# Expert rows kept as planes of half words and turned into columns by the load's DMA transpose, instead of by TensorE

## The chip, the cores and the metric

The kernel runs on one core of a Trainium2 chip as one launch. The metric is the device time of one execution in microseconds (us); the time of before is the median of three runs. Besides, one execution was recorded by the profiler, and every duration below comes from that one. Engines carry the names of the profile: PE is TensorE (PEld its weight loads), ACT is ScalarE, DVE is VectorE, POOL is GpSimd, SP is SyncE, which here only issues DMAs.

## The reference, cut to what matters

```python
x = attention(q, k, v)                     # 4 batches x 576 tokens, 8 heads of 64: 2304 rows of 512
x = (x @ w_a) * (x @ w_b) @ w_out          # 512 -> 1536 -> 512
en = expert_emb / (norm(expert_emb) + 1e-6)            # 8 experts
logits = (x / (norm(x) + 1e-6)) @ en.T / tau
expert_idx = argmax(logits, axis=1)
gate_w = softmax(logits)[rows, expert_idx]
for e in range(8):
    mask = expert_idx == e
    out[mask] = gate_w[mask, None] * (relu(x[mask] @ w1[e]) @ w2[e])   # 512 -> 1024 -> 512
```

All of it is fp32. The kernel gets fp32 products out of three matmuls each: an operand is split into a high part (rounded, `fp32r`) and a low part (what the rounding left), and `mm3` adds high x high, high x low and low x high.

## The kernel before

**Stages.** Four blocks of tokens pass through attention and the first feed-forward part (`f_step`, twelve steps per block, and `x1_run` for the product with `w_out`); the attention of the next block is woven into the steps of the current one. While a block's steps run, the rows of the block before it are routed (`Router`): logits on DVE, the choice of the expert, the rank within the expert on PE, and then `scatter`, an indirect DMA from POOL that puts each token's row into the DRAM table `xs` at a slot of its expert. A row there is 521 words: 512 of x, 8 logit differences, the token's number. The last block is done in columns (`x1_last`: twelve steps for 512 tokens, twelve for the other 256); its routers `ra` (4 tiles of 128 tokens) and `rb` (2 tiles) get the rows by matmuls against an identity, `row_out` copies them from PSUM with ACT.

**The experts** (`Moe2`) come in the order of their load, with capacities of 384, 352, 336, 320, 304, 288, 272 and 256 tokens. For one expert `x_load` brings the rows back as `xr` (tokens on the partitions), and `x_prep` makes columns of them: PE transposes 128x128 pieces against the identity into PSUM (`x_trans`, L1052), `split` makes the high part `xTh` with ACT (L679) and the low part `xTl` with DVE (L680). For expert 0 this is `x_early` (256 tokens, while block 3 still runs) and `x_rest`. `h_full` multiplies with w1 (eight pieces, into PSUM tiles `hp`, three buffers), `y_part` or, for the experts in `TURNED`, `yt_part` with w2. `y_out` scales by the gate and scatters to the output. `gate_sq` takes the sum of squares of each row tile with ACT's Square (L1085), `gate` makes the inverse norm on DVE and the softmax's sum with one Exp on ACT (L1094).

**Order.** The program's order is written by hand and each engine works through its own instructions in that order; nothing is rescheduled. SP issues every load in one queue: weight pieces of 512 KB (`w_load`), four ahead of the one that `w_split` takes apart, and the rows of expert e+2 (`x_load`) when expert e is done. `GATE_AT` says behind which `yt_part` the gate's instructions stand, `XPREP` which columns of the next expert are made behind which.

Of the kernel before, what the change touches and what calls it, by code (L numbers as in the profile page):

```python
# [12 lines left out]
U32 = mybir.dt.uint32  # L13
AF = mybir.ActivationFunctionType
# [5 lines left out]
E, F2 = 8, 1024  # L20
# [17 lines left out]
GATE_AT = 0  # L38
# [6 lines left out]
RW = DM + E + 1  # L45
C_DL = DM
C_IDX = DM + E
# [13 lines left out]
MASK_OF = {0: 0, 2: 2, 4: 3, 6: 4, 7: 5}  # L61

# [20 lines left out]
def fused_kernel(ctx: ExitStack, tc: tile.TileContext, qk, v, wab, wout, w1, w2, emb, tau, cst, msk, out, dbg=None):  # L83
# [5 lines left out]
    xs = dram.tile([E * RS, RW], F32, name="xs")  # L89
# [78 lines left out]
    def make_empty():  # L168
        empty = rbox[0][:, NTT:NTT + 1, :]
        nc.gpsimd.memset(empty, 0.0)  # L170
        nc.gpsimd.memset(empty[:, :, C_IDX:], SENT)
        return empty

    def prefill(empty, e):
        nc.sync.dma_start(
            out=xs[e * RS:e * RS + CAP, :].rearrange("(t p) c -> p t c", p=128),
            in_=empty.to_broadcast([128, NCT, RW]),
        )
# [5 lines left out]
    class Router:  # L184
        def __init__(self, tile0, nt, rows, x, ps, tags):
# [20 lines left out]

        def row_out(self, t, h):
            p = self.pr.pop((t, h))
# [61 lines left out]
        def scatter(self, t):  # L270
            i = nc.gpsimd.indirect_dma_start(
                out=xs, out_offset=bass.IndirectOffsetOnAxis(ap=self.di[:, t:t + 1], axis=0),
                in_=self.rows[:, t, :], in_offset=None,
# [7 lines left out]
        def steps(self, per):  # L281
# [9 lines left out]
            for _ in range(3):  # L291
                yield
# [684 lines left out]
    class Moe2:  # L977
# [4 lines left out]
        def __init__(self):  # L982
# [4 lines left out]
            self.xr, self.ixi, self.xT, self.hT, self.sq, self.gates = {}, {}, {}, {}, {}, {}  # L987
# [46 lines left out]
        def x_load(self, e, t0=0, t1=None):  # L1034
# [3 lines left out]
            if e not in self.xr:  # L1038
                self.xr[e] = self.mr.tile([128, NCT, RW], F32, tag="xr", name="xr", bufs=2)[:, :self.nct(e), :]
# [3 lines left out]
                self.sq[e] = rt.tile([128, NCT], F32, tag="sq", name="sq")[:, :self.nct(e)]  # L1043
                self.gates[e] = self.mr.tile([128, NCT], F32, tag="gate", name="gate", bufs=3)[:, :self.nct(e)]
            nc.sync.dma_start(
                out=self.xr[e][:, t0:t1, :], in_=xs3[self.expert(e), 128 * t0:128 * t1, :].rearrange("o (t p) c -> p (o t) c", p=128))

        def x_ids(self, e, t0, t1):
            nc.vector.tensor_copy(out=self.ixi[e][:, t0:t1], in_=self.xr[e][:, t0:t1, C_IDX])

        def x_trans(self, e, tp, d, t, c):
            nc.tensor.transpose(tp[:, c:c + 128], self.xr[e][:, t, 128 * d:128 * d + 128], ident)  # L1052

        def x_prep(self, e, ds):
            if e >= E:
                return
            if 0 in ds:
                self.x_ids(e, 0, self.nct(e))
            for d in ds:
                if e == 1:  # L1060
                    tp = self.pt.tile([128, CAP], F32, tag="hp", name="xtq", bufs=3)
                else:
                    tp = self.pt.tile([128, 512], F32, tag="xtp", name="xtp")
                for t in range(self.nct(e)):
                    self.x_trans(e, tp, d, t, 128 * t)
                split(tp[:, :CAPS[e]], self.xT[e][0][:, d, :], self.xT[e][1][:, d, :])

        def x_early(self, h):
            tp = ps.tile([128, 2, EARLY], F32, tag=f"mm{2 + h}", name="xte")
            for d in range(2):  # L1070
                for t in range(EARLY // 128):
                    self.x_trans(0, tp[:, d, :], 2 * h + d, t, 128 * t)
            split(tp, *[x[:, 2 * h:2 * h + 2, :EARLY] for x in self.xT[0]])

        def x_rest(self):
            m = CAPS[0] - EARLY
            tp = self.pt.tile([128, 4, 128], F32, tag="xtp", name="xtr")[:, :, :m]
            for d in range(4):
                self.x_trans(0, tp[:, d, :], d, EARLY // 128, 0)
            split(tp, *[x[:, :, EARLY:] for x in self.xT[0]])  # L1080

        def gate_sq(self, e, t):
            if t < self.nct(e):
                jk = self.mr.tile([128, DM], BF16, tag="jk", name="jk")
                nc.scalar.activation(out=jk, in_=self.xr[e][:, t, :DM], func=AF.Square, accum_out=self.sq[e][:, t:t + 1])  # L1085

        def gate(self, e):
            n = self.nct(e)
            sh = [128, n, E]
            ri = inv_norm(self.sq[e], 128, n)  # L1090
            dl = rt.tile([128, NCT, E], F32, tag="dl", name="dl")[:, :n, :]
            g = self.gates[e]
            nc.vector.tensor_tensor(out=dl, in0=self.xr[e][:, :, C_DL:C_DL + E], in1=ri.unsqueeze(2).to_broadcast(sh), op=ALU.mult)
# [3 lines left out]
            nc.vector.reciprocal(out=g, in_=g)  # L1097

# [41 lines left out]

        def h_full(self, e):
            c0, c1 = 0, CAPS[e]
            for f in range(8):
# [4 lines left out]
                if 1 <= f <= 3:  # L1148
                    self.yt_turn(e - 1, f - 1)
                    self.gate_sq(e, f - 1)  # L1150
                if f == 5 and e not in TURNED:
                    self.gate(e)
# [49 lines left out]
        def run(self):  # L1202
# [3 lines left out]
            for t in range(self.nct(0)):  # L1206
                self.gate_sq(0, t)
            self.h_rest()
            self.gate(0)
            for e in range(E):  # L1210
# [3 lines left out]
                if e in TURNED:  # L1214
                    for d in range(4):
# [3 lines left out]
                        if d == GATE_AT:  # L1219
                            self.gate(e)  # L1220
# [381 lines left out]
```

## Time and profile before

| | |
|---|---|
| time, median of 3 runs | 782.15 us (780.53 to 783.88) |
| the profiled execution: its time | 778.46 us |
| the profiled execution: its span | 776.6 us |
[...]
| PE busy | 765.0 us, 99% |
| DVE, ACT, POOL busy | 507.9, 403.1, 206.1 us |
| DMA | 138.45 MB, mean 178 GB/s |

The span runs from the first to the last instruction; the 1.9 us between it and the execution's time lie around it. A share of busy time says how full an engine is on average, not whether something waits for it.

### The profile page before, as it was taken

The numbers are of one execution on the slowest core, as the hardware profiler recorded it, in microseconds if no ns is written. First come the engines' busy times: TensorE is split into PE (matmuls) and PEld (weight loads), VectorE is DVE, ScalarE is ACT, GpSimd is POOL, SyncE is SP. The second block draws the span as 40 slices with busy tenths as digits, with TensorE's granted clock in tenths as the row PEclk, the third lists the DMA queues.
The fourth block names the chain that finished last, engine by engine and source line by source line (L and its number), as shares of the span: only waits on it lengthen the run. The fifth ranks groups of instructions, "written<-read, shape, count | busy, mean of one in ns | idle before, by whom it ended". The sixth has DMA issues, their size and how long they took to land.

```text
span 776.6 us, 14562 instructions
## 1 busy us (share of the span) xinstructions
PE 765.0 (99%) x5503; PEld 683.0 (88%) x5503; DVE 507.9 (65%) x1072; ACT 403.1 (52%) x945; POOL 206.1 (27%) x228
## 2 busy tenths in 40 slices
PE   7999999999999999999999999999999999999997
PEld 4799998888788888888899998899897999999995
DVE  4788878758895388975376743355565565665672
ACT  5776764367642366642333332455463554755761
POOL 3634443023521234342032324421011000101111
PEclk9999999999999999999999999999999999999999
DMA  9968779478752433213512123444574545645621
GB/s 353 370 223 274 247 272 336 147 274 285 287 193 81 164 116 132 83 55 100 173 55 82 55 82 144 184 138 162 210 252 161 184 155 167 231 154 197 234 81 37
DMA packets 40672, 138.45 MB, mean 178 GB/s; under 512 B 4082, under 2 KB 4338, under 8 KB 38160
## 3 DMA queue, kind: packets, MB, share of 16 engines
q1 hardware_dynamic: 37504, 127.90, 48.0%
q0 software_dynamic: 3088, 9.52, 3.2%
q8 instruction: 45, 0.74, 0.4%
q14 instruction: 35, 0.29, 0.1%
HBM read 112.03 MB, written 25.80 MB: 177 GB/s over the span
## 4 chain that ended last, share of the span: by engine, by line
PE 86%; issue 5%; DMA 4%; DVE 2%; ACT 1%; POOL 1%; POOLq 0%; DVEq 0%; ACTq 0%
PE mm L721 13%; PE mm L723 12%; PE mm L722 12%; PE xr L721 4%; PE xr L723 4%; PE xr L722 4%; DMA out_dram<-yo,ixi 4%; PE hp L721 3%; PE hp L723 3%; PE hp L722 3%; PE xm L721 2%; PE xm L723 2%; PE xm L722 2%; PE ytp L723 2%; PE ytp L722 2%
## 5 line engine op out<-in xcount | busy, mean ns | idle before, releaser
L721 PE MATMUL mm<-x0h,ab 128*128 128x288 f32 (+2 forms) x480 | 171.1, 357 | 0.0
L723 PE MATMUL mm<-x0h,ab 128*128 128x288 f32 (+2 forms) x480 | 166.9, 348 | 0.2 <-DVE ab L680 0.2
L722 PE MATMUL mm<-x0l,ab 128*128 128x288 f32 (+2 forms) x480 | 166.8, 347 | 0.2 <-DVE x0l L506 0.2
L680 DVE TENSOR_TENSOR wl<-raw,wh 128x1024 fp32r<-128x1024 f32 x60 | 73.0, 1222 | 53.6 <-ACT wh L679 53.5
L776 POOL TENSOR_TENSOR gl<-g,gh 128x288 fp32r<-128x288 f32 (+2 forms) x60 | 82.2, 1370 | 84.9 <-ACT gh L775 81.5
L721 PEld LDWEIGHTS mm<-x0h,ab 128*128 128x128 f32 x480 | 90.2, 188 | 10.0
L723 PEld LDWEIGHTS mm<-x0h,ab 128*128 128x128 f32 x480 | 90.1, 188 | 9.6 <-DVE ab L680 0.4
L722 PEld LDWEIGHTS mm<-x0l,ab 128*128 128x128 f32 x480 | 90.2, 188 | 8.5 <-DVE x0l L506 0.5
L680 DVE TENSOR_TENSOR wo<-wor,wo 128x512 fp32r<-128x512 f32 x60 | 43.9, 731 | 58.2 <-ACT wo L679 54.5
L679 ACT ACTIVATE wo<-wor 128x512 fp32r<-128x512 f32 x60 | 37.9, 631 | 84.4 <-PE xr L723 52.7
L1192 POOL DMA_INDIRECT out_dram<-yo,ixi x23 | 24.4, 1062 | 207.6 <-ACT yo L1191 164.7
L680 DVE TENSOR_TENSOR ab<-abr,ab 128x1024 fp32r<-128x1024 f32 x45 | 59.3, 1318 | 24.9 <-ACT ab L679 24.9
L772 DVE TENSOR_TENSOR g<-a,mm 128x288 f32<-128x288 f32 (+2 forms) x72 | 39.5, 549 | 51.8 <-PE mm L723 42.0
L721 PE MATMUL hp<-xTh,wh 128*128 128x352 f32 (+6 forms) x224 | 69.0, 308 | 0.0
L723 PE MATMUL hp<-xTh,wl 128*128 128x352 f32 (+6 forms) x224 | 67.7, 302 | 0.0
L722 PE MATMUL hp<-xTl,wh 128*128 128x352 f32 (+6 forms) x224 | 67.6, 302 | 0.0
L679 ACT ACTIVATE wh<-raw 128x1024 fp32r<-128x1024 f32 x64 | 67.0, 1054 | 0.0
L775 ACT ACTIVATE gh<-g 128x288 fp32r<-128x288 f32 (+2 forms) x60 | 33.1, 552 | 57.5 <-DVE g L772 57.5
L679 ACT ACTIVATE ab<-abr 128x1024 fp32r<-128x1024 f32 (+1 forms) x53 | 50.6, 961 | 17.5 <-PE mm L723 11.9
L223 DVE SCALAR_TENSOR_TENSOR jl<-rows,en_a 128x512 bf16<-128x512 f32 x60 | 56.2, 937 | 1.2
L721 PE MATMUL xr<-wo,gh 128*128 128x512 f32 x144 | 56.4, 392 | 0.0
L723 PE MATMUL xr<-wo,gl 128*128 128x512 f32 x144 | 56.1, 390 | 0.0
(262 smaller groups left out, 1793.0 us busy)
## 6 DMA issues: line engine op xcount, KB each, us to landing
raw<-in_w_dram SPq DMA_DIRECT2D x64, 512.0 KB
abr<-wab SPq DMA_DIRECT2D x36, 512.0 KB
wor<-wout SPq DMA_DIRECT2D x24, 512.0 KB
qkt<-in_qk_dram SPq DMA_DIRECT2D x12, 832.0 KB
vt<-in_v_dram SPq DMA_DIRECT2D x12, 768.0 KB
c<-in_wab_dram SPq DMA_DIRECT2D x8, 1024.0 KB
xs<-rows SPq DMA_DIRECT2D x8, 781.5 KB
wab<-abr SPq DMA_DIRECT2D x12, 512.0 KB
```

Of the source, the lines that this page charges most:

```text
L223: nc.vector.scalar_tensor_tensor(out=jl, in0=self.rows[:, t, :DM], scalar=1.0, in1=ebox[e // E1][:, e % E1, :], op0=ALU.mult, op1=ALU.mult ...
L679: nc.scalar.activation(out=hi, in_=raw, func=AF.Copy)
L680: (eng or nc.vector).tensor_tensor(out=lo, in0=raw, in1=hi.bitcast(F32), op=ALU.subtract)
L721: nc.tensor.matmul(out=out_, lhsT=lh, rhs=rh, start=first, stop=False)
L722: nc.tensor.matmul(out=out_, lhsT=lh, rhs=rl, start=False, stop=False)
L723: nc.tensor.matmul(out=out_, lhsT=ll, rhs=rh, start=False, stop=last)
L772: nc.vector.tensor_tensor(out=g, in0=kept[hf], in1=acc[1, hf], op=ALU.mult)
L775: nc.scalar.activation(out=hi, in_=g, func=AF.Copy)
L776: nc.gpsimd.tensor_tensor(out=lo, in0=g, in1=hi.bitcast(F32), op=ALU.subtract)
L1192: nc.gpsimd.indirect_dma_start(out=out, out_offset=bass.IndirectOffsetOnAxis(ap=self.ixi[e][:m, t:t + 1], axis=0), in_=yo[:m, :], in_offse ...
```

## The change

A row in `xs` has 524 words now. Its 512 words of x stand as two planes of 16-bit halves: 512 low halves, then 512 high halves. Behind them come the logit differences, two words for the sum of squares (`C_SQ`), the token's number and one spare word. `x_load` issues a DMA transpose of the planes, which puts them as columns into `pl` (128 partitions, 8 groups, tokens), and a small DMA for the 12 words behind (`tl`). `x_join` puts the halves together again with one ACT copy of 16-bit elements into `xf`, and `split` takes the parts from there. The TensorE transposes and their PSUM tiles go.

On the side of the rows, POOL writes the planes of a tile into the neighbouring slot of the row buffer (`planes`), ACT takes the squares (`square`), and `scatter` first copies the 12 words to that slot. In `rb` ACT writes the planes straight from PSUM. `gate` is cut in two: its DVE part stands behind the first `yt_part`, its Exp and the rest behind the third. `x_early` moves from steps 17 and 20 of `x1_last` to steps 9 and 11.

```diff
-GATE_AT = 0
+GATE_AT = (0, 2)
-RW = DM + E + 1
+RW = DM + E + 4
 C_DL = DM
-C_IDX = DM + E
+C_SQ = DM + E
+C_IDX = DM + E + 2
+PLANE_AT = (21, 23, 25, 27)
...
+        def square_row(self, t):
+            if self.x is None:
+                junk = self.stage[t][:, :DM // 2].bitcast(BF16)
+            else:
+                junk = rt.tile([128, DM], BF16, tag="jl", name="jl", bufs=1)
+            self.square(t, self.rows[:, t, :DM], 0, junk)
+
+        def planes(self, t, eng):
+            out = self.stage[t % len(self.stage)][:, :DM].bitcast(U16).rearrange("p (w c) -> p w c", w=2)
+            in_ = self.rows[:, t, :DM].bitcast(U16).rearrange("p (c w) -> p w c", w=2)
...
+                eng.tensor_copy(out=out, in_=in_)
...
         def row_out(self, t, h):
+            halves = self.rows[:, t, :DM].bitcast(U16).rearrange("p (w k c) -> p w k c", w=2, k=4)
             nc.scalar.activation(
-                out=self.rows[:, t, 256 * h:256 * h + 256].rearrange("p (k c) -> p k c", k=2),
-                in_=p[:, :, :128], func=AF.Copy)
+                out=halves[:, :, 2 * h:2 * h + 2, :],
+                in_=p.bitcast(U16).rearrange("p k (c w) -> p w k c", w=2), func=AF.Copy)
+            jl = rt.tile([128, DM], BF16, tag="jl", name="jl", bufs=1)
+            self.square(t, p, h, jl[:, :256])
...
         def logit(self, i):
             t, e = divmod(i, E)
+            if i in PLANE_AT:
+                q = PLANE_AT.index(i)
+                self.square_row(q)
+                self.planes(q, nc.gpsimd)
...
         def scatter(self, t):
+            row = self.rows[:, t, :]
+            if self.stage:
+                row = self.stage[t % len(self.stage)]
+                nc.gpsimd.tensor_copy(out=row[:, DM:], in_=self.rows[:, t, DM:])
...
+            r0, r1 = 128 * t0, min(128 * t1, CAPS[e])
+            nc.sync.dma_start_transpose(
+                out=self.pl[e][:, :, r0:r1], in_=xs3[self.expert(e), r0:r1, :DM].bitcast(U16).rearrange("o r c -> (o r) c"))
             nc.sync.dma_start(
-                out=self.xr[e][:, t0:t1, :], in_=xs3[self.expert(e), 128 * t0:128 * t1, :].rearrange("o (t p) c -> p (o t) c", p=128))
+                out=self.tl[e][:, t0:t1, :], in_=xs3[self.expert(e), 128 * t0:128 * t1, DM:].bitcast(F32).rearrange("o (t p) c -> p (o t) c", p=128))
...
-        def x_trans(self, e, tp, d, t, c):
-            nc.tensor.transpose(tp[:, c:c + 128], self.xr[e][:, t, 128 * d:128 * d + 128], ident)
+        def x_join(self, e, d0, d1, r0, r1):
+            n = d1 - d0
+            x = self.mr.tile([128, 2 * CAP], U32, tag="xf", name="xf", bufs=2)[:, :n * (r1 - r0)]
+            x = x.rearrange("p (d c) -> p d c", d=n)
+            words = x.bitcast(U16).rearrange("p d (c w) -> p w d c", w=2)
+            planes = self.pl[e].rearrange("p (w d) c -> p w d c", w=2)[:, :, d0:d1, r0:r1]
+            nc.scalar.activation(out=words, in_=planes, func=AF.Copy)
+            split(x.bitcast(F32), *[y[:, d0:d1, r0:r1] for y in self.xT[e]])
...
-        def gate_sq(self, e, t):
-            if t < self.nct(e):
-                jk = self.mr.tile([128, DM], BF16, tag="jk", name="jk")
-                nc.scalar.activation(out=jk, in_=self.xr[e][:, t, :DM], func=AF.Square, accum_out=self.sq[e][:, t:t + 1])
...
+                    if 15 <= i < 15 + ha:
+                        ra.square_row(i - 15)
+                        ra.planes(i - 15, nc.gpsimd)
-                    if i == 18:
-                        for t in range(ha):
-                            ra.scatter(t)
-                    if i in (17, 20):
-                        moe.x_early((i - 17) // 3)
+                    if 18 <= i < 18 + ha:
+                        ra.scatter(i - 18)
+                    if i in (9, 11):
+                        moe.x_early((i - 9) // 2)
```

Three places show what stands where. PE, in expert 1's products with w2 (`yp`), where the columns of expert 2 are made; before:

```order
L723 MATMUL yp<-wh,hTl 128x512
L1052 MATMUL xtp<-ident,xr 128x128 x6
L721 MATMUL yp<-wh,hTh 128x512
L722 MATMUL yp<-wl,hTh 128x512
L723 MATMUL yp<-wh,hTl 128x512
```

and there is nothing in place of the six transposes afterwards:

```order
L764 MATMUL yp<-wh,hTl 128x512
L762 MATMUL yp<-wh,hTh 128x512
L763 MATMUL yp<-wl,hTh 128x512
L764 MATMUL yp<-wh,hTl 128x512
L762 MATMUL yp<-wh,hTh 128x512
```

The transposes have left PE's list. SP's queue, where expert 0 is done: `raw` are weight pieces, `xr` the rows of expert 2; before:

```order
L1010 DMA raw<-in_w_dram 128x1024
L1010 ISA
L1010 DMA raw<-in_w_dram 128x1024
L1045 ISA
L1045 DMA xr<-xs 128x3x521
L1010 ISA
L1010 DMA raw<-in_w_dram 128x1024
```

and afterwards, at the same place, with `pl` for the planes and `tl` for the words behind them:

```order
L1051 DMA raw<-in_w_dram 128x1024
L1051 ISA
L1051 DMA raw<-in_w_dram 128x1024
L1087 ISA
L1087 DMA_TRANSPOSE pl<-xs 128x8x336
L1089 ISA
L1089 DMA tl<-xs 128x3x12
L1051 ISA
L1051 DMA raw<-in_w_dram 128x1024
```

The transposed load takes the place of the plain one, between the same weight pieces, and a second DMA follows it. ACT, where the rows of the last two tiles (`rowsb`) come out of PSUM between the first products of expert 0 (`hTh` from `hpe`); before:

```order
L959 ACTIVATE x1b<-xm_5557 128x512
L1109 ACTIVATE hTh<-hpe 128x256
L209 ACTIVATE rowsb<-rps 128x256 x2
L1109 ACTIVATE hTh<-hpe 128x256
L209 ACTIVATE rowsb<-rps 128x256 x2
L1109 ACTIVATE hTh<-hpe 128x256 x2
```

and afterwards:

```order
L1000 ACTIVATE x1b<-xm_5603 128x512
L1144 ACTIVATE hTh<-hpe 128x256
L240 ACTIVATE rowsb<-rps 128x2x256
L216 ACTIVATE jl,rowsb<-rps 128x256
L240 ACTIVATE rowsb<-rps 128x2x256
L216 ACTIVATE jl,rowsb<-rps 128x256
L1144 ACTIVATE hTh<-hpe 128x256
L240 ACTIVATE rowsb<-rps 128x2x256
L216 ACTIVATE jl,rowsb<-rps 128x256
L240 ACTIVATE rowsb<-rps 128x2x256
L216 ACTIVATE jl,rowsb<-rps 128x256
L1144 ACTIVATE hTh<-hpe 128x256 x2
```

Each of the four copies has twice the elements (16-bit ones), and a Square follows each.

## Rows read from the trace of the kernel before

**Rows 1.** The page: span, busy time, granted clock, the load queue.

```profile
span 776.6 us, 14562 instructions
PE 765.0 (99%) x5503; PEld 683.0 (88%) x5503; DVE 507.9 (65%) x1072; ACT 403.1 (52%) x945; POOL 206.1 (27%) x228
...
PEclk9999999999999999999999999999999999999999
...
q1 hardware_dynamic: 37504, 127.90, 48.0%
```

**Rows 2.** Stretches: length; PE, PEld, DVE, ACT, POOL busy; PEclk, DMA share, GB/s.

```profile
601.83:632.59 30.76, 30.76 (x205) 30.73 (x204) 18.41 (x42) 16.14 (x31) 0.95 (x1) 1.00 0.44 146
...
540.00:776.60 236.60, 231.13 (x1550) 219.84 (x1548) 139.16 (x335) 126.60 (x248) 25.48 (x25) 1.00 0.51 172
...
547.00:553.00 6.00, 6.00 (x30) 4.90 (x28) 3.07 (x16) 3.25 (x8) 0.00 (x0) 1.00 1.03 413
```

**Rows 3.** Chain that ended last: start us, us, what.

```profile
547.01 0.44 PE xtr L1052 x4
...
589.58 0.66 PE xtp L1052 x6
```

**Rows 4.** Busy time of line 1052 over the span (PE, then PEld).

```profile
0.00:776.60 776.60, 12.81 (x92) 10.93 (x92) 1.00 0.52 178
```

**Rows 5.** ACT by shape: count, busy us, mean ns, idle before.

```profile
L679 ACT ACTIVATE wh<-raw 128x1024 fp32r<-128x1024 f32 x64 | 67.0, 1054 | 0.0
L679 ACT ACTIVATE wo<-wor 128x512 fp32r<-128x512 f32 x60 | 37.9, 631 | 84.4 <-PE xr L723 52.7 <-PE xm L722 23.4 <-issue 3.7
L1085 ACT ACTIVATE jk<-xr 128x512 bf16<-128x512 f32 x23 | 14.4, 628 | 0.1
L1085 ACT ACTIVATION_READ_ACCUMULATOR jk<-xr 128x1 f32 x23 | 4.5, 198 | 0.0
L209 ACT ACTIVATE rowsb<-rps 128x256 f32<-128x256 f32 x4 | 1.4, 384 | 2.5 <-PE rk L252 1.1 <-DVE lg L205 0.8 <-DVE lg L202 0.6
L1130 ACT ACTIVATE hr<-hrp 128x512 f32<-128x512 f32 x2 | 1.2, 598 | 4.4 <-PE hrp L723 4.4
```

**Rows 6.** Waits over the span: us in total, times, longest.

```profile
ACT dl L1094 <- DVE dl L1093: 33.6, 7, 5.0
```

**Rows 7.** POOL by shape: count, busy us, mean ns, idle before.

```profile
L680 POOL TENSOR_TENSOR wl<-raw,wh 128x1024 fp32r<-128x1024 f32 x4 | 9.7, 2427 | 18.6 <-ACT wh L679 15.5 <-issue 3.1
L160 POOL COPY id_en<-ident 128x128 f32<-128x128 f32 x4 | 3.9, 1026 | 0.0
...
L1361 POOL CAST xel<-x0l 128x512 fp32r<-128x512 f32 x1 | 0.6, 609 | 0.0
```

**Rows 8.** Timeline where the last rows are routed: PE's rank, POOL's scatters.

```profile
535.99 0.18 PE L249 MATMUL rk<-oh,u_bf 128*128 128x16 bf16 x1 [0.17 <-DVE oh L239]
...
538.78 0.96 POOL L271 DMA_INDIRECT xs<-rowsb,di  x1 [12.79 <-ACT hTh L1109]
...
540.05 0.97 POOL L271 DMA_INDIRECT xs<-rowsb,di  x1 [0.21 <-issue]
```

**Rows 9.** Timeline where `x1T` is copied: ACT, and PE's next use of the accumulators.

```profile
506.25 2.64 ACT L955 ACTIVATE x1T<-xm 128x512 f32<-128x512 f32 x4 [0.28 <-PE xm L723]
...
508.09 0.28 PE L721 MATMUL xm<-geh,wo 128*128 128x256 f32 x1
```

**Rows 10.** Timeline of SP: issues of row loads.

```profile
542.87 1.54 SPq L1045 DMA_DIRECT2D xr<-xs  x2
...
605.49 0.39 SPq L1045 DMA_DIRECT2D xr<-xs  x1
```

**Rows 11.** Timeline: ACT's first split of expert 1's and 3's columns, PE's first use.

```profile
559.03 0.80 ACT L679 ACTIVATE xTh<-xtq 128x352 fp32r<-128x352 f32 x2
...
621.73 0.76 ACT L679 ACTIVATE xTh<-xtp 128x320 fp32r<-128x320 f32 x2
...
568.36 0.32 PE L721 MATMUL hp<-xTh,wh 128*128 128x352 f32 x1
```

More of the change, by code (lines that the diff above doesn't have):

```diff
@@ L184, in fused_kernel, with __init__ @@
     class Router:
-        def __init__(self, tile0, nt, rows, x, ps, tags):
+        def __init__(self, tile0, nt, rows, x, ps, tags, stage=None):
+            self.stage = stage
             self.tile0, self.nt, self.rows, self.x, self.ps, self.tags = tile0, nt, rows[:, :nt, :], x, ps, tags
@@ L270, in scatter @@
         def scatter(self, t):
+            row = self.rows[:, t, :]
+            if self.stage:
+                row = self.stage[t % len(self.stage)]
+                nc.gpsimd.tensor_copy(out=row[:, DM:], in_=self.rows[:, t, DM:])
             i = nc.gpsimd.indirect_dma_start(
                 out=xs, out_offset=bass.IndirectOffsetOnAxis(ap=self.di[:, t:t + 1], axis=0),
-                in_=self.rows[:, t, :], in_offset=None,
+                in_=row.bitcast(U32), in_offset=None,
             )
@@ L290, in steps @@
             self.choose()
-            for _ in range(3):
+            for k in range(3):
                 yield
@@ L1037, in x_load @@
             t1 = self.nct(e) if t1 is None else t1
-            if e not in self.xr:
-                self.xr[e] = self.mr.tile([128, NCT, RW], F32, tag="xr", name="xr", bufs=2)[:, :self.nct(e), :]
+            if e not in self.pl:
+                self.pl[e] = self.mr.tile([128, 8, CAP], U16, tag="pl", name="pl", bufs=2)
+                self.tl[e] = self.mr.tile([128, NCT, RW - DM], F32, tag="tl", name="tl", bufs=2)[:, :self.nct(e), :]
                 p = self.mr if e % 2 == 0 else self.ml
@@ L1058, in x_prep @@
                 self.x_ids(e, 0, self.nct(e))
[L1059 to L1066, printed above, removed]
-        def x_early(self, h):
[L1069 to L1073, printed above, removed]
-        def x_rest(self):
[L1076 to L1080, printed above, removed]
-        def gate_sq(self, e, t):
-            if t < self.nct(e):
-                jk = self.mr.tile([128, DM], BF16, tag="jk", name="jk")
-                nc.scalar.activation(out=jk, in_=self.xr[e][:, t, :DM], func=AF.Square, accum_out=self.sq[e][:, t:t + 1])
+            self.x_join(e, ds[0], ds[-1] + 1, 0, CAPS[e])
+        def x_early(self, h):
+            self.x_join(0, 2 * h, 2 * h + 2, 0, EARLY)
+        def x_rest(self):
+            self.x_join(0, 0, 4, EARLY, CAPS[0])
         def gate(self, e):
@@ L1205, in run @@
             self.x_ids(0, 0, self.nct(0))
-            for t in range(self.nct(0)):
-                self.gate_sq(0, t)
             self.h_rest()
-            self.gate(0)
+            list(self.gate(0))
             for e in range(E):
@@ L1214, in run @@
                 if e in TURNED:
+                    gate = self.gate(e)
                     for d in range(4):
@@ L1218, in run @@
                         self.x_prep(e + 1, XPREP[d])
-                        if d == GATE_AT:
-                            self.gate(e)
+                        if d in GATE_AT:
+                            next(gate)
                 if e == E - 1:
@@ L1230, in run @@
                         self.w_split()
-                    if t < 2:
+                    if t < 2 and (e or t):
                         self.x_prep(e + 1, [2 * t, 2 * t + 1])
@@ L1367, in fused_kernel @@
                     empty = make_empty()
-                router = Router(NTT * b, NTT, rbox[0], None, ps, ["rps"])
+                router = Router(NTT * b, NTT, rbox[0], None, ps, ["rps"], [rbox[0][:, (t - 1) % (NTT + 1), :] for t in range(NTT)])
             else:
@@ L1378, in fused_kernel @@
                 endx_ctx.close()
-                ra = Router(NTT * b, ha, rbox[0], xbox[0], ps, ["rps", "sc", "tp", "av"])
+                ra = Router(NTT * b, ha, rbox[0], xbox[0], ps, ["rps", "sc", "tp", "av"], [rbox[0][:, (t - 1) % (NTT + 1), :] for t in range(NTT)])
                 moe = Moe2()
@@ L1470, in fused_kernel @@
                     w2s = lp.tile([128, 8, DM], F32, tag="w2s", name="w2s")
-                    nc.sync.dma_start(out=xs[bass.ds(e_r * RS + n_r, LATE), :], in_=free)
+                    nc.sync.dma_start(out=xs[bass.ds(e_r * RS + n_r, LATE), :].bitcast(F32), in_=free)
                     nc.sync.dma_start(out=w1s, in_=w1[bass.ds(e_r, 1), :, :].rearrange("o (k p) f -> p (o k) f", p=128))
```

58 lines of the change are left out of this document (40 added, 18 removed).

## The prediction

> **What bounds the kernel now.** I read the page first: PE is busy for 99% of the span at a granted clock of 1.0 throughout, and no other engine is above 65% [rows 1]. So PE is the bound by average, but an average can hide a stage with another limit, so I then looked at the stage that the change touches. From 540 us on PE is busy 231.1 of 236.6 us, and most of the rest is the end of the program; in expert 2's stretch it is busy for all of 30.76 us, while ACT has 16.1 and DVE 18.4 us of work there, and DMA is used for 44% of it [rows 2]. The chain of work that ended last shows the TensorE transposes themselves as pieces of it [rows 3]. What leaves PE there is therefore a gain, as long as nothing that takes its place comes late.
>
> **What goes.** There are 92 transposes [rows 4]. In the chain six together stand for 0.66 us and four for 0.44 us, the slow start of the matmul behind them included [rows 3]. Experts 1 to 6 have two groups of six each, expert 0 has three groups of four and expert 7 two: 12 x 0.66 + 5 x 0.44 = 10.1 us. (Their busy time of 12.81 us in [rows 4] counts overlapping tails.) ACT also loses 23 Squares with their read-outs, 628 + 198 ns each [rows 5].
>
> **What ACT gets.** An `x_join` of two groups for 336 tokens copies 1,344 16-bit elements. No row shows a 16-bit copy; between 512 and 1,024 elements from SBUF ACT takes 631 and 1,054 ns, 0.83 ns per element [rows 5], which gives 1.32 us, at most twice that if halves cost extra. Two joins per expert are 2.6 us (5.3 at most), and the split after them costs what it did, about 1.5 us. The three Squares that go are 2.5 us. So ACT stays near 16 of 30.8 us, and it has more room than this says: it stood 33.6 us in seven gates, up to 5.0 us each, before an Exp that waits for DVE's chain [rows 6], and the cut gate puts two `yt_part`s between the two. I cost this at nothing; the cover is ACT's idle half, and at 5.3 us it is still there. DVE's instructions stay the same in kind and number, nearly.
>
> **What the rows' side gets.** In the earlier blocks each tile has a Square (0.83 us on ACT) and a copy of 1,024 16-bit elements on POOL, whose price no row shows: 1.2 us at the pace of the 512-element cast (609 ns), 2.4 us like the 1,024-element subtraction, 8.2 us at the pace of the 128-element copy (1,026 ns) [rows 7]. I take 2 us, since the cast is the plain one-input case and the 128-element copies ran at the start, beside other work. Queued behind it on POOL are the low parts of g, which PE wants only when `x1_run` reaches that step, some 25 us later, and the ACT instruction that waits for POOL is the next Square, whose junk goes into the slot being copied. PE has a second pair of accumulators there. I cost it at nothing up to 5 us a copy.
>
> **Seams.** Three places have little cover.
> (a) `rb`. ACT writes the rows as 512 elements from PSUM (598 ns as `hr` does) instead of 256 (384 ns), and takes a Square of 256 with a read-out, about 0.4 + 0.2 us behind it [rows 5]. Two of these stand ahead of the relu of expert 0's second product, whose low part on DVE stands ahead of the choice of the expert. That chain grows by about 1.0 us, and PE's rank matmul already waits 0.17 us for it [rows 8]: +1.0 us.
> (b) `x_early` at step 11 puts a join and a high part, 1.7 us, ahead of the copies of `x1T`, whose first accumulator PE wants back at 508.09; the copies start at 506.25, and the first is done by 506.9 [rows 9]. With the 0.3 us that ACT idles there 1.5 us are to spare: +0.3 us for this copy and those behind it.
> (c) `x_rest`, below.
>
> **The transposed load.** This is the unknown. A plain load moves 2 KB rows at 413 GB/s when the engines are full [rows 2], so 336 rows (688 KB) take 1.7 us. The transposed one reads the same bytes, as 8 pieces of 256 bytes a row if it works by columns of 128 halves: 2,688 pieces. A packet of the load queue took 48.0% x 776.6 x 16 / 37,504 = 159 ns for 3.4 KB on average [rows 1]; if each piece cost that, the load would take 2,688 x 159 / 16 = 26.7 us. At 413 / 16 = 25.8 bytes per ns a packet's bytes account for 132 of its 159 ns, so 27 ns are its own; a piece of 256 bytes then costs 27 + 10 = 37 ns and the load 6.2 us. I take 6.2 and keep 1.7 and 26.7.
> What covers it: expert 3's rows are asked for at 605.49 and ACT splits them at 621.73 [rows 10, 11]; the other experts from 2 on have as much or more. So 16 us are free, the landing of about 2 us included (the scatter that POOL issues until 541.0 releases the load at 542.87, [rows 8, 10]). At 6.2 us nothing waits, and the DMA engines go from 51% [rows 2] to 63%. The load for `x_early` has some 9 us of slack at the new place. In (c) the last 128 rows of expert 0 are asked for at 542.87 [rows 10] + 1.0, need 2.0 + 2.4 us to land and a join and a high part of 1.7 us: 550.0 us. PE's four transposes stand at 547.01 [rows 3], with about 2.1 us of products between them and the use of these columns; without them it gets there at 549.1, and at 549.4 with the 1.3 us of (a) and (b) and without the 0.9 us of `x_early`'s transposes: +0.6 us (at 26.7 us for a whole load it would be +8).
> [...]
>
> **Sum.** -10.1 + 1.0 + 0.3 + 0.6 = -8.2 us. Against its own execution that is 778.5 to 770.3 us. The median of the three runs stands 3.7 us above the profiled execution, inside their spread of 780.5 to 783.9; I carry the difference over: **774 us**. A measurement here tells about 0.5% from nothing, 3.9 us.
>
> **Rivals.**
> *Loads at the packet's price (slower).* If every 256-byte piece costs a whole packet's 159 ns, the 2,256 rows loaded after 540 us take 2,256 x 8 x 159 / 16 = 179 us of all DMA engines. They are busy 0.51 x 236.6 = 121 us there now, 14 of it for the plain rows: 286 us in a stretch of 237, so the program ends some 50 us later, about 835 us. It decides from about 14 us of transfer for 320 rows, where the split of the weights behind the load in SP's queue comes late too. For it: no row shows short pieces. Against it: packets here spend their time on bytes. [...]
> *Seams eat the gain (no change).* At 80 ns a piece an expert's load takes 13 us and the steady stretches still hide it; but 128 rows take 5 us at (c), +3 us, and expert 1's 352 rows, 14 us right behind, land at about 565, when ACT wanted them at 559 and PE needs them split at 568 [rows 11], with both joins and splits, some 5 us, and weights behind them on ACT: +4 us. -8.2 + 2.7 + 4, about 780.5 us.
> *POOL's copies are slow.* `ra`'s four copies can start at about 513, some 4 us behind the `x1T` copies [rows 9], and four scatters follow, 1.27 us apart as `rb`'s two are, with their small copies 6.8 us by my estimate; the scatter of `rb` wants POOL at 538.8, where it now starts [rows 8]. That gives 25.8 us, so a copy may take 4.7 us. At 8.2 us `rb`'s rows leave 14 us late, the last rows of expert 0 with them, and PE stands for it: about 788 us. Against it: the cast's row.
> *The load as cheap as a plain one* and joins without any stall: 772 us; this lies within my own case.
>
> **How the numbers follow.** My case, 771 to 777 us, gets 0.57; the seams 0.17; the packet's price 0.15; POOL 0.05; 0.06 for what I do not see, on either side. The prediction is that of my case. The range leaves out the packet's price and takes in the rest: 769.5 to 789 us, some 0.82. Faster by over 0.5% (below 778.2) holds my case, a third of the seams and half of the unseen: 0.66. Within 0.5%: most of the seams, 0.14. Slower: the packet's price and POOL, 0.20.
>
> **What would show it.** PE without line 1052 and its stretch from 540 us to its last matmul about 7 us shorter. A wait of PE at the rank of about 1.2 us and one of about 0.6 us in front of `hrp`. ACT's joins near 1.3 us for 336 tokens without a DMA as what ended the idle time before them: if ACT waits for `pl` in the experts 2 to 7, the load is the bound and I am wrong; if it waits only in experts 0 and 1, the seams rival holds. POOL's plane copies near 2 us; at over 5 us POOL's last scatter is late. I would also be wrong if the Squares and copies in the blocks before 480 us made PE wait; PE's busy share there should stay as it is.

## The result and the profile after

The changed kernel takes **772.19 us** (median of four runs, 771.72 to 773.08) against 781.78 us for the kernel before (median of four, 780.53 to 783.88): a ratio of 0.9876, with a 95% interval of 0.9852 to 0.99. On a second chip, where both were timed again, it was 771.95 us (six runs) against 779.44 us (eighteen): 0.9901, interval 0.9878 to 0.9924. The time forecast was 774.0 us, within 769.5 to 789. So it is faster by 7.5 to 9.6 us; the sum said 8.2.

The page of the profile after, the lines that answer to [rows 1]:

```profile
span 770.8 us, 14427 instructions
PE 756.9 (98%) x5411; PEld 673.8 (87%) x5411; DVE 514.9 (67%) x1067; ACT 428.5 (56%) x942; POOL 229.6 (30%) x261
...
PEclk9999999999999999999999999999999999999999
...
q1 hardware_dynamic: 57888, 127.09, 50.5%
```

PE has exactly 92 matmuls fewer, ACT is 25 us fuller and POOL 24. The load queue has 20,384 packets more and only 2.5 points more of the engines' time: the short pieces of the transposed loads are there, and they are cheap.

The stretches that answer to [rows 2] (expert 2's, and from 540 us to the end; columns as there):

```profile
601.89:631.34 29.45, 29.45 (x194) 29.45 (x192) 17.50 (x38) 17.84 (x25) 0.95 (x1) 1.00 0.54 141
540.00:770.80 230.80, 224.47 (x1485) 213.29 (x1484) 141.57 (x344) 140.05 (x206) 27.79 (x27) 1.00 0.59 172
```

Expert 2's stretch was 30.76 us and is 29.45: two groups of six transposes for 1.31 us, PE still busy for all of it. ACT went from 16.1 to 17.8 us there.

PE's waits from 480 us to the end (us in total, times, longest); before, the list had one row, 0.2 us at the rank:

```profile
PE xm L764 <- DVE wo L721: 1.3, 1, 1.3
PE rk L286 <- DVE oh L276: 0.6, 1, 0.6
PE hp L763 <- DVE xTl L721: 0.3, 1, 0.3
PE xm L762 <- ACT x1T L996: 0.2, 1, 0.2
PE hpe L762 <- DVE hTl L1145: 0.2, 1, 0.2
```

The largest, in `x1_last`, is in no step of the prediction. Ahead of that the blocks run as before: from 60 to 480 us PE is busy for 419.9 of 420 us (420.0 before). What the new instructions cost, by shape, ACT's and then POOL's (count, busy us, mean ns, idle before):

```profile
L1101 ACT ACTIVATE xf<-pl 128x1024 uint16<-128x1024 uint16 x5 | 6.8, 1369 | 2.7 <-DMA pl<-xs 2.7
L1101 ACT ACTIVATE xf<-pl 128x1408 uint16<-128x1408 uint16 x2 | 3.6, 1818 | 0.0
L1101 ACT ACTIVATE xf<-pl 128x1344 uint16<-128x1344 uint16 x2 | 3.5, 1727 | 0.0
L240 ACT ACTIVATE rowsb<-rps 128x512 uint16<-128x512 uint16 x4 | 2.4, 598 | 2.0 <-DVE lg L211 0.8 <-DVE lg L208 0.6 <-DVE rowsb L280 0.5
...
L231 POOL COPY rows<-rows 128x1024 uint16<-128x1024 uint16 x16 | 19.1, 1191 | 17.8 <-ACT rows L216 6.5 <-ACT rows L236 6.1 <-issue 4.2
```

Only one of the seventeen joins waited for a load (2.7 us). The transposed loads on SP's queue and that join on ACT (start us, us):

```profile
549.42 1.37 ACT L1101 ACTIVATE xf<-pl 128x1024 uint16<-128x1024 uint16 x1 [2.74 <-DMA pl<-xs]
...
545.76 1.24 SPq L1087 DMA_TRANSPOSE pl<-xs  x1
548.40 2.82 SPq L1087 DMA_TRANSPOSE pl<-xs  x1
574.88 5.17 SPq L1087 DMA_TRANSPOSE pl<-xs  x1
```

SP itself is held for 1.2 to 7.3 us by the issue of one such load; a plain one takes it 0.4 us. From issue to landing, where the traces show it, a transposed load takes 9.3 us in the changed kernel and 4.8 to 9.1 us, with a median of 6.9 us, in double_load (below); the wait of ACT's join for the 128 rows ended 3.7 us after their load was issued (545.76 to 549.42).

**One clock for all traces.** The start of a program varies: PE reached the router's total (`cpl`, one matmul in block 3) between 474.3 and 475.5 us in all traces but one. From that row on PE's times repeat within 0.03 us from trace to trace of one kernel but for two places where 0.1 us came or went (both named below), so places are compared as distances from it. The rows, of the kernel before, then of the second trace of the changed kernel (`after_again`):

```profile
475.32 0.18 PE L305 MATMUL cpl<-hs,ones_bf 128*128 128x8 bf16 x1
509.51 2.02 PE L195 MATMUL rps<-id_en,x1T 128*128 128x136 f32 x16
529.57 0.28 PE L721 MATMUL hpe<-xTh,wh 128*128 128x256 f32 x1
770.73 0.40 PE L723 MATMUL yp<-wh,hTl 128*128 128x512 f32 x1
```

```profile
474.97 0.18 PE L346 MATMUL cpl<-hs,ones_bf 128*128 128x8 bf16 x1
509.65 2.02 PE L201 MATMUL rps<-id_en,x1T 128*128 128x136 f32 x16
530.96 0.28 PE L762 MATMUL hpe<-xTh,wh 128*128 128x256 f32 x1
551.32 0.39 PE L762 MATMUL hrp<-wh,xTh 128*128 128x512 f32 x1
569.02 0.32 PE L762 MATMUL hp<-xTh,wh 128*128 128x352 f32 x1
763.93 0.39 PE L764 MATMUL yp<-wh,hTl 128*128 128x512 f32 x1
```

The same distances for every kernel that is used below (us from the start of `cpl` to the start of the first row of each kind; the last column to the end of the last matmul):

| kernel | rps | hpe | hrp | hp, expert 1 | hp, expert 2 | end of PE |
|---|---|---|---|---|---|---|
| before | 34.19 | 54.25 | 74.07 | 93.04 | 126.51 | 295.81 |
| changed (after_again) | 34.68 | 55.99 | 76.35 | 94.05 | 126.35 | 289.35 |
| tr_back | 34.68 | 56.00 | 76.80 | 95.81 | 129.04 | 298.33 |
| place_late | 34.66 | 54.56 | 74.90 | 92.60 | 124.99 | 287.98 |
| planes_twice | 34.67 | 58.43 | 78.80 | 96.49 | 128.78 | 291.77 |
| early79 | 34.22 | 55.54 | 75.88 | 93.59 | 125.90 | 288.89 |
| sq_late | 34.68 | 55.99 | 75.62 | 93.32 | 125.63 | 288.62 |
| gate_one | 34.67 | 55.98 | 76.34 | 94.04 | 126.34 | 301.67 |
| all4 | 34.22 | 54.10 | 73.71 | 91.42 | 123.60 | 286.60 |

Read along the first two lines: the changed kernel is behind by 0.5 us at `rps`, 1.7 at `hpe`, 2.3 at `hrp`, has made that up by expert 2, and ends 6.46 us ahead. The first trace of the changed kernel lost another 0.1 us between `hrp` and expert 1.

### The profile page after: what moved, and what is told of

The parts are those of the page before. It is cut to its first block, busy times and chain, and to the rows that moved or that the text cites. A ratio compares the mean times of both kernels' runs of the same rounds, so it can differ in the third digit from the quotient of the medians.

```text
span 770.8 us, 14427 instructions
## 1 busy us (share of the span) xinstructions
PE 756.9 (98%) x5411; PEld 673.8 (87%) x5411; DVE 514.9 (67%) x1067; ACT 428.5 (56%) x942; POOL 229.6 (30%) x261
## 4 chain that ended last, share of the span: by engine, by line
PE 85%; DMA 4%; issue 3%; ACT 3%; DVE 3%; POOL 0%; POOLq 0%; SPq 0%; DVEq 0%; ACTq 0%
PE mm L762 13%; PE mm L764 13%; PE mm L763 12%; PE xr L763 4%; PE xr L762 4%; PE xr L764 4%; PE hp L763 4%; PE hp L764 4%; PE hp L762 4%; PE ytp L764 3%; PE ytp L762 3%; PE ytp L763 2%; PE xm L762 2%; PE xm L764 2%; PE xm L763 2%
## 5 line engine op out<-in xcount | busy, mean ns | idle before, releaser
L260 DVE SCALAR_TENSOR_TENSOR jl<-rows,en_a 128x512 bf16<-128x512 f32 x60 | 58.9, 982 | 1.2
L762 PE MATMUL xr<-wo,gh 128*128 128x512 f32 x144 | 56.4, 392 | 0.0
L763 PE MATMUL xr<-wo,gh 128*128 128x512 f32 x144 | 56.2, 390 | 0.1
```

The source lines that it names most:

```text
L260: nc.vector.scalar_tensor_tensor(out=jl, in0=self.rows[:, t, :DM], scalar=1.0, in1=ebox[e // E1][:, e % E1, :], op0=ALU.mult, op1=ALU.mult ...
L762: nc.tensor.matmul(out=out_, lhsT=lh, rhs=rh, start=first, stop=False)
L763: nc.tensor.matmul(out=out_, lhsT=lh, rhs=rl, start=False, stop=False)
```

## The experiments

**tr_back: the transposes put back.**

```diff
         def x_prep(self, e, ds):
+            for d in ds:
+                tp = self.pt.tile(...)
+                for t in range(self.nct(e)):
+                    nc.tensor.transpose(tp[:, 128 * t:128 * t + 128], ident, ident)
             self.x_join(e, ds[0], ds[-1] + 1, 0, CAPS[e])
...
         def x_rest(self):
+            tp = self.pt.tile([128, 4, 128], F32, tag="xtp", name="xtr")
+            for d in range(4):
+                nc.tensor.transpose(tp[:, d, :], ident, ident)
             self.x_join(0, 0, 4, EARLY, CAPS[0])
```

> The changed kernel with 84 of the 92 TensorE transposes issued again at their old places (of the identity into a PSUM tile that nobody reads; the eight of the early load stay out). Theory, the gain is PE's own work: the stretches between the same points of the two traces were 9.1 us shorter where these 84 groups went, so the time goes from 772.2 to about 781. Rival, the gain comes from elsewhere (the Squares that left ACT, the cut gate): PE has some slack to take the transposes in, and the time stays below 776.

781.23 us, ratio to before 1.0018 (1.0001 to 1.0035), and PE ends 8.98 us later than in the changed kernel. So the gain is PE's own time, and nothing there took the transposes in. The eight that stayed out are two groups of four; in the kernel before each delays the matmul behind it by 0.35 or 0.36 us, and that one takes 0.08 us longer than usual until the next starts, 0.88 us for both. So the 92 are worth 9.86 us; the prediction had 10.1.

**plain_load and double_load: the price of the transposed load.**

```diff
# plain_load (experts 1 to 7)
-            nc.sync.dma_start_transpose(out=self.pl[e][:, :, r0:r1], in_=...)
+            nc.sync.dma_start(out=<pl[e], a row of 1024 halves per partition and tile>, in_=...)
# double_load
             nc.sync.dma_start_transpose(out=self.pl[e][:, :, r0:r1], in_=...)
+            if e > 1:
+                nc.sync.dma_start_transpose(out=pl2[:, :, r0:r1], in_=...)
```

> The changed kernel with plain loads in place of the transposed ones for experts 1 to 7 (same rows, same bytes, 2 KB pieces; the joined words are then rows and not columns, so what the experts compute is not the reference's). Theory, the transposed load is hidden everywhere: within 0.5 us of 772.2, and SP's issues of these loads fall from 3 to 7 us to about 0.4 us. Rival, the load still costs something that no single wait shows (DMA share, weights queued behind its long issue): 1 to 3 us faster, 769 to 771.

> The changed kernel with a second transposed load of the same rows (into a tile that nobody reads) right behind the first for experts 2 to 7. By the prediction's cover of some 16 us and a load that takes 6 to 9 us, a second one is still hidden: 772 to 774, with SP busy 3 to 5 us longer at each place. Rival, the load already stands close to its limit of 14 us or holds back the weights queued behind it on SP: PE waits for the weights' split or for the columns in each of the experts 2 to 7, at 2 us or more each, 780 to 790.

771.84 and 771.83 us, and PE's distances are those of the second trace of the changed kernel within 0.03 us, up to its end. The load is hidden, and so is a second one. One stretch of the three kernels, from 575 to 750 us (length; PE, PEld, DVE, ACT, POOL busy; PEclk, DMA share, GB/s): plain, as changed (`after_again`), doubled.

```profile
575.00:750.00 175.00, 175.00 (x1226) 171.20 (x1225) 112.60 (x258) 113.36 (x168) 20.86 (x17) 1.00 0.56 187
```

```profile
575.00:750.00 175.00, 175.00 (x1225) 171.20 (x1224) 112.76 (x258) 113.33 (x168) 17.91 (x17) 1.00 0.63 183
```

```profile
575.00:750.00 175.00, 175.00 (x1226) 171.20 (x1225) 112.18 (x258) 113.16 (x169) 19.67 (x17) 1.00 0.73 203
```

The second set of loads (1,776 rows, at 8 pieces of 256 bytes each 14,208 pieces; the page after has 20,384 packets more for 2,512 rows, 8.1 a row) raises the share by 0.10, or by 0.08 against the first trace's 0.65 of the same stretch. That is 14.0 to 17.5 us of all 16 engines: 16 to 20 ns a piece, 2.6 to 3.3 us for 336 rows. The other pair gives more: from plain to transposed the share rises by 0.07 (0.09 against the first trace), 12 to 16 us, on top of what the plain loads took in it. By the 413 GB/s of [rows 2] their 4.46 MB are 10.8 us, an estimate, so that the first set costs 23 to 27 us: 26 to 30 ns a piece, 4.4 to 5.0 us for 336 rows. The prediction took 37 ns and 6.2 us, with 1.7 and 26.7 as bounds.

**place_late and planes_twice: PE's wait in x1_last.** PE's new wait of 1.3 us had two candidates. In the changed kernel DVE's rows around it (start us, us) and POOL's:

```profile
519.67 0.18 DVE L297 TENSOR_TENSOR pk<-rk,c_sb 128x32 f32<-128x32 f32 x1
519.88 0.82 DVE L298 TENSOR_TENSOR pk<-pk,oh 128x32 f32<-128x32 f32 x1
520.73 0.19 DVE L299 TENSOR_REDUCE df<-pk 128x4 f32<-128x32 f32 x1
...
521.26 1.00 DVE L305 TENSOR_TENSOR hs<-hs,hsum 128x8 bf16<-128x8 bf16 x1
522.19 1.28 DVE L721 TENSOR_TENSOR wo<-wor,wo 128x512 fp32r<-128x512 f32 x2
```

```profile
519.61 1.04 POOL L231 COPY rows<-rows 128x1024 uint16<-128x1024 uint16 x1 [0.41 <-ACT jl L216]
521.21 1.04 POOL L231 COPY rows<-rows 128x1024 uint16<-128x1024 uint16 x1 [0.55 <-ACT jl L216]
```

Two DVE instructions of 0.2 us take 0.82 and 1.00 us, and each ends within 0.05 us of the end of a plane copy on POOL (520.65, 522.25). Behind them stands the low part of the weights (`wo`) that PE waits for.

```diff
# place_late
                     if i == 16:
                         ra.rank()
+                    if i == 19:
                         ra.place()
                         ra.total()
-                    if 18 <= i < 18 + ha:
-                        ra.scatter(i - 18)
+                    if 20 <= i < 20 + ha:
+                        ra.scatter(i - 20)
# planes_twice
-                        ra.planes(i - 15, nc.gpsimd)
+                        for _ in range(2):
+                            ra.planes(i - 15, nc.gpsimd)
```

> The changed kernel with DVE's place and total of the four tiles behind step 19 instead of 16 and the four scatters two steps later; ACT's Squares and POOL's plane copies stay where they are. Theory A, POOL's plane copies hold up the DVE instructions beside them (two-input ones took 0.82 and 1.00 us there instead of 0.19 and 0.17), and the split queued behind them came late: with place and total out of the way PE's wait of 1.3 us at 522.9 us goes or falls below 0.4, and the time falls by 1 to 2 us, to 770.2 to 771.2. Theory B, ACT's Squares ahead of its half of the split make it late: the wait stays above 1 us and the time at 772.2.

> The changed kernel with POOL's plane copies of the four tiles in the last block made twice each. Theory, a copy of 1.04 us holds up DVE's two-input instructions beside it: with eight copies in a row DVE's place, total and split wait for more of them, PE's wait at 522.9 us grows from 1.3 us to between 2 and 5 us, and the time rises by as much. Rival, the wait comes from ACT's Squares: unchanged at 1.3 us, since ACT does nothing more.

place_late: 770.56 us, 1.4 us less at `hpe` and at PE's end, and PE's wait for `wo` is gone. The same two instructions there, clear of the copies:

```profile
523.80 0.19 DVE L298 TENSOR_TENSOR pk<-pk,oh 128x32 f32<-128x32 f32 x1
...
524.56 0.17 DVE L305 TENSOR_TENSOR hs<-hs,hsum 128x8 bf16<-128x8 bf16 x1
```

planes_twice: 774.58 us, and PE's longest wait grew from 1.3 to 2.0 us. ACT has the same work in both, so theory B (the Squares) falls, and A stands: POOL's copy holds DVE up. With six copies in a row a conversion, which has one input, is held up as well (0.17 us without a copy); the two reductions beside them are not:

```profile
520.37 0.19 DVE L299 TENSOR_REDUCE df<-pk 128x4 f32<-128x32 f32 x1
520.59 0.83 DVE L300 CAST di<-df 128x4 int32<-128x4 f32 x1
521.33 0.19 DVE L304 TENSOR_REDUCE hsum<-oh 128x8 f32<-128x32 bf16 x1
...
517.71 7.75 POOL L231 COPY rows<-rows 128x1024 uint16<-128x1024 uint16 x6 [3.36 <-issue]
```

But `hpe` is 2.44 us later than in the changed kernel, and the longer wait is only 0.7 us of that. Most of the rest came behind the wait, where PE slowed down:

```profile
523.17 0.39 PE L764 MATMUL xm<-geh,wo 128*128 128x256 f32 x1 [2.03 <-DVE wo L721]
...
524.55 0.42 PE L762 MATMUL xm<-geh,wo 128*128 128x256 f32 x1
524.77 0.42 PE L763 MATMUL xm<-gel,wo 128*128 128x256 f32 x1
```

From 524.3 to 527.7 us these matmuls start 0.21 us apart instead of 0.12; that is some 1.5 us more. In gate_one (below) a like stretch, 0.23 us apart instead of 0.13, goes with a granted clock of 0.50; what the clock was in this one is not shown. So the 2.44 us are no measure of what the copies themselves cost.

Which instructions of DVE the copies held up, the rows show as far as this: beside the copies those with two inputs in SBUF were held up (0.82 for 0.19 us, 1.00 for 0.17), while the first of the list above, whose `rk` lies in PSUM, was not (0.18), nor were the one-input reductions of planes_twice (0.19). The conversion that was held up (0.83 for 0.17) has one input. What decides it no run here shows.

**early79 and sq_late: the two seams that were foreseen.**

```diff
# early79
-                    if i in (9, 11):
-                        moe.x_early((i - 9) // 2)
+                    if i in (7, 9):
+                        moe.x_early((i - 7) // 2)
# sq_late: in row_out the Square goes, and
         rb.choose()
+        <Squares of the first halves>
         for t in range(hb):
             rb.row_out(t, 1)
         moe.h_early(range(2, H_MID))
+        <Squares of the second halves>
```

> The changed kernel with the two early joins at steps 7 and 9 of the last block instead of 9 and 11. Theory, the join at step 11 stands ahead of the copies of x1T on ACT and costs PE the 0.8 us by which it reaches the first 256-column product later (508.8 us against 508.1 before, from the same place at 480 us): PE's wait for x1T goes and the time falls by 0.6 to 0.8 us, to 771.4 to 771.6. Rival, the rows of the early load have not landed by step 7 (the load was issued from 482.9 us on and its issue alone took 7.3 us): ACT waits for them there, with the weights' split behind it, and the time stays or rises.

> The changed kernel with the four Squares of the last two tiles moved: the first two behind the second relu of expert 0, the other two behind the third. Theory, the Squares are what makes the chain to the rank longer by the 0.5 us that PE loses there, and the third relu late by another 0.5 us: both waits of PE (0.63 and 0.17 us) shrink and the time falls by 0.5 to 1.0 us. Rival, the copies of 512 halves (0.60 us against 0.38 before) make the chain late by themselves: the waits stay and the time is 772.

early79: 771.41 us; `rps` comes at 34.22 instead of 34.68, as before the change, so the join at step 11 cost 0.46 us. The rows had landed: no join waited there. sq_late: 770.87 us; PE's wait at the rank fell from 0.6 to 0.3 us, that for `hTl` went, and `hrp` comes 0.73 us earlier. So most of the loss at `rb` is the Squares' place; the 0.2 to 0.3 us that are left were not traced further, the wider copies being one candidate.

**gate_one: the gate in one piece again.**

```diff
-GATE_AT = (0, 2)
+GATE_AT = (0,)
...
                         if d in GATE_AT:
-                            next(gate)
+                            list(gate)
```

> The changed kernel with the gate in one piece again, behind the first part of the product with w2. Theory, the gate's wait on ACT lies in ACT's idle time: ACT waits for DVE's dl seven times again, some 30 us in all instead of 9, and the time stays within 0.5 us of the changed kernel. Rival, with the joins ACT is full enough that the waits reach PE (columns late for the next expert, or PSUM tiles not freed): 1 to 5 us slower.

The rival holds, and by more than it said: **782.80 us**, 10.9 us slower than the changed kernel and slower than before (ratio 1.0036, 1.0021 to 1.005). PE's waits in this run:

```profile
PE hp L762 <- ACT xTh L720: 4.8, 5, 1.5
PE hp L763 <- DVE xTl L721: 2.2, 6, 0.4
```

ACT in expert 2's second product, with the next expert's columns behind the gate:

```profile
622.69 0.74 ACT L720 ACTIVATE xTh<-xf 128x640 fp32r<-128x640 f32 x1
628.01 0.22 ACT L1128 ACTIVATE dl<-dl 128x24 f32<-128x24 f32 x1 [4.58 <-DVE dl L1126]
...
629.42 1.68 ACT L1101 ACTIVATE xf<-pl 128x1280 uint16<-128x1280 uint16 x1
631.12 0.74 ACT L720 ACTIVATE xTh<-xf 128x640 fp32r<-128x640 f32 x1
```

The Exp stands 4.6 us for DVE's chain, as before the change ([rows 6]). Then it cost nothing: the split alone stood behind it (0.75 us). Now a join of 1.7 us stands ahead of the split, and expert 3's first product, which PE starts at 630.53 us, wants the high part that ends at 631.9. From the start of one expert's `hp` to the next (for the last, to PE's end) the experts 3, 4 and 5 take 1.3, 1.6 and 1.9 us longer so, the experts 6 and 7 3.7 and 3.9 us. Some 2 us of each of the last two have another cause: PE had waited 1.27 and 1.51 us there, each time with a second wait of 0.3 to 0.4 us close behind. Behind the first of them (columns as before):

```profile
722.50:724.00 1.50, 1.50 (x7) 1.50 (x8) 1.11 (x1) 1.50 (x4) 0.00 (x0) 0.50 0.74 283
...
726.00:728.00 2.00, 2.00 (x18) 2.00 (x17) 0.69 (x2) 1.63 (x3) 0.00 (x0) 1.00 0.82 258
```

The granted clock is 0.50 here, 0.54 from 724 to 726 us and 1.00 again from 726 us on; behind the second of the two waits it is 0.50 from 753.5 to 755.5 us. Behind the waits of 1.05 us and less it stayed at 1.00. In the changed kernel, with the gate cut, ACT waits for `dl` for 9.2 us in two gates; here it is 31.7 us in seven.

**all4 (and all4_again): what the experiments point to.** place_late, early79 and sq_late together, and expert 1's second join ahead of two weight splits:

```diff
+                    if t < 2 and e == 0 and t:
+                        self.x_prep(e + 1, [2 * t, 2 * t + 1])
                     self.w_split()
                     if t == 0 or e == 0:
                         self.w_split()
-                    if t < 2 and (e or t):
+                    if t < 2 and e:
                         self.x_prep(e + 1, [2 * t, 2 * t + 1])
```

> The changed kernel with four edits of order together: place, total and scatters later (measured alone at 770.6), the early joins at steps 7 and 9, the Squares of the last two tiles later, and expert 1's second join ahead of the two weight splits that stood before it. If the losses read in the trace (1.9, 0.8, 1.0 and 0.4 us) are separate and all of them come back, 768.1; if the last one only moves the wait to the weights, 768.5. Rival, the seams hide one another, so that only the largest counts: 770 to 770.6.

> The four edits of order together, once more, beside the changed kernel on one chip: 2.5 to 3.0 us less than that. If the earlier difference (769.3 against 772.2) came from two chips, less than 1.5 us.

769.27 us, and 769.61 us beside the changed kernel's 771.95 on one chip: 2.3 us less by the medians and 2.75 us by PE's end (2.64 in the trace of all4_again), where the three single edits add to 2.56 (1.37 + 0.46 + 0.73). So the losses are separate, but smaller than the 4.1 us that the expectation had read for the four; the kernel is faster than both others. One wait of PE is left from 480 us on, 0.3 us at the rank. The second join gave nothing clear: from expert 1 to expert 2 it is 32.18 us in one trace and 32.29 in the other, instead of 32.30.

**before_again and after_again: the traces themselves.**

> The kernel before, once more, with a profile of its own: the one at hand lasted 778.5 us and lies below all of its 19 later timings (779.4 to 784.9, median 780.2). If that profile was an early finish by chance, the new one lasts about 780 and the two traces of before differ by 1.5 us or more in some stretch that the change doesn't touch; if a profiled execution is shorter by itself, it lasts 778.5 again.

> The changed kernel once more, on the chip of the next three. Its first profile had a lower granted clock between 10 and 20 us; from the router's total at 475 us on the two traces should agree within 0.2 us, and the time should be 771.3 to 772.5.

after_again is the table's second line; it was timed at 771.95 us. before_again: 779.91 us, but its profiled execution lasted 784.7, neither of the two cases named. It reached `cpl` at 481.37 us, 6 us late, and from there on agrees with the first trace within 0.01 us at every place of the table. Where it was late:

```profile
20.00:30.00 10.00, 8.90 (x97) 6.36 (x97) 7.11 (x22) 7.19 (x43) 6.51 (x12) 0.54 0.85 316
```

The granted clock was 0.54 in these ten microseconds of the first block, which the change doesn't touch, and 1.00 there in the first trace. So what sets these two traces of the kernel before apart lies at the start of its program.

## Why the prediction was right, point by point

**The transposes, -10.1 us:** right in kind (tr_back) and nearly in size, -9.86. A group of six is worth 0.66 us where it can be read alone (1.31 us for two in expert 2).

**(a) rb, +1.0:** from `hpe` to `hrp` the changed kernel takes 20.36 us and the one before 19.82 with `xtr` in it, which tr_back prices at 0.44 (20.80 against 20.36): +0.98. Place and size were right, but the wait at the rank (0.6) was half of what was named (1.2); a wait for the next relu's low part (`hTl`, 0.2) was not named, and the rest shows as no wait.

**(b) x_early, +0.3:** the place was right and the cost a little more, +0.46 (early79) to +0.49 (at `rps`).

**(c) x_rest, +0.6:** no wait of PE shows there. The load was issued 2.9 us later than before (545.76 against 542.87, [rows 10]), not 1.0, and landed 3.7 us after its issue (4.4 assumed); ACT, which had nothing else to do, waited 2.7 us of that. But PE came to `hrp` 2.3 us later too. Both hang on what went before: the load waits for `rb`'s scatter, which waits for PE's rank, so what PE loses or saves in front moves the load as well. The prediction took the 0.9 us of `x_early`'s transposes off PE's way to `hrp` and not off the load's. all4 bears this out: without the losses in front PE's rank comes 2.3 us earlier (60.61 us after `cpl` against 62.89) and `hrp` 2.6 us earlier, and again PE doesn't wait for these columns.

**The step that was missing, +2.13:** the prediction costed POOL's plane copies "at nothing up to 5 us a copy", with their time on POOL (2 us assumed, 1.04 us each in `ra`) and the queues behind them as the only way to cost something; that a copy holds up DVE stands nowhere in it. From `rps` to `hpe` the kernel before takes 20.06 us, 19.18 without its transposes, and the changed one 21.31. place_late gets 1.4 us of it back. Most of the other 0.7 us is the pace of the single products: the 256-column matmuls of this stretch start 0.120 us apart on average, before 0.115 (0.113 behind the transposes). The cause of that is open.

**Joins, 1.32 us for 1,344 elements:** they take 1.73 us. The slope between 1,024 and 1,408 elements is 1.17 ns an element, not 0.83; the bound of twice was wide enough.

**ACT's joins, costed "at nothing":** the result holds, the reason doesn't. The cover named was ACT's idle half; gate_one shows that this half, lying in front of the gate's Exp, covers nothing for what stands behind it. The cut gate is the cover, and without it the change would have been slower than before. The prediction named the cut in half a sentence and gave no price for its absence: that was the rival on the other side that it should have worked out.

**The transposed load, 6.2 us:** 2.6 to 5.0 us of all engines by the two pairs above, so both rivals that rest on it (the packet's price, the seams) fall, and doubling it still cost nothing. The time from issue to landing is another number: a median of 6.9 us in double_load and 9.3 at most, where the loads of plain_load, seven of nine plain, have a median of 5.7. That is near the 8.2 us that the prediction allowed with its 2 us of landing, and well inside the 16 us of cover. For the 3.64 MB of the 1,776 rows the two pairs give 14 to 27 us of all engines, 137 to 260 GB/s.

**The sum:** -9.86 + 0.98 + 0.49 + 0.0 + 2.13 = -6.26, and PE's end moved by -6.46. Two errors, a missed 2.13 and a (c) that was 0.6 too dear, partly cancel against 8.2. The medians moved by more, 7.5 us on one chip. The remaining 1.0 us lies outside the stretch from `cpl` to PE's end: ahead of `cpl`, where the traces of before stand at 475.3 and 481.4 us and the two of the changed kernel at 475.4 and 475.0, or behind PE's end, where before has 5.5 and 5.6 us left and the changed kernel 5.9 and 5.4. Whether the start is more often late in the one is not settled. Two more errors lie in the forecast of 774 and work against each other: the trace moved by 1.7 us less than the sum, and the 3.7 us by which before's median stood above its profile was carried over, while the changed kernel's median lies 0.4 us below its own. That 774 came within 2 us of 772.19 is therefore in part luck.

## What to carry to other kernels

An engine's idle share covers new work only if that work can be done in the idle time: look for the one long stand in its queue, and price the work that is put behind it, since what stands behind a wait gets nothing from the time lost in it (in gate_one ACT stood 4.6 us, and PE then waited up to 1.5 us for the split behind it). A copy on POOL that is hidden on POOL can still be paid for by DVE (0.82 and 1.00 us for 0.19 and 0.17 beside copies of 1.04 us); look at what DVE does in the same microsecond, not only at who waits for the copy. And a distance from a late common row shows a few tenths of a microsecond that medians with a noisy start can't: here the distances repeat within 0.03 us but for two places, and before's times on one chip range from 778.1 to 784.6 us.

## What the hardware showed unexpectedly

The issue of a transposed load holds SP for 1.2 us (128 rows) to 7.3 us (256 rows, the first); the loads of weights queued behind it on SP had to wait for that, and PE's times stayed the same, even with two transposed loads in a row. A plane copy on POOL of 1.04 us held up DVE instructions of 0.17 to 0.19 us to 0.82 and 1.00 us. Waits of PE of 1.27 and 1.51 us in gate_one, each with a second one of 0.37 and 0.34 us close behind, were followed by some 3 us at a granted clock of 0.5, and one of 2.03 us in planes_twice by 3.4 us in which the matmuls started 0.21 us apart instead of 0.12. One of 1.32 us alone in `x1_last` of the changed kernel was not, nor one of 1.05 us with 0.40 us behind it in gate_one (granted clock 1.00 behind both). So the length of a single wait does not tell the cases apart.
